# First four blocks of a windowed attention: products of the exponentials in float32 on TensorE instead of split 16-bit values through a DMA transpose; one normalization per half block

## The chip, the cores and the metric

One core of a Trainium2 chip runs the whole program. The metric is device microseconds of one execution; three executions of the kernel before stand at 866.73, 866.99 and 868.85 us.

The engines are PE (TensorE, matrix products; PEld is its loading of the stationary operand), DVE (VectorE), ACT (ScalarE), POOL (GpSimd) and SP (SyncE, which here only issues DMAs). Each runs its own instructions strictly in program order; they wait for one another by semaphores.

## The reference, cut to what matters

```python
# attention: 4 sequences, 8 heads, 576 positions, 64 columns a head
scores = q @ k.T / 8 + slopes[h] * -(i - j)     # where 0 <= i - j < 128, else -1e9
attn = exp(scores - max); attn = attn / (sum(attn) + 1e-9)
x = attn @ v                                    # as 2304 tokens x 512
# dense layer
h = x @ w_in; g = h - tanh(h); x = g @ w_out    # 512 -> 2048 -> 512
# eight experts, each token to the one with the largest cosine
out[token] = gate * (relu(x @ w1[e]) @ w2[e])   # 512 -> 1024 -> 512
```

All of it is float32. Which expert a token goes to hangs on small differences, so the kernel carries nearly all of its products in float32 accuracy, most of them as three products of values split in a high and a low part.

## The kernel before, in words

The 2304 tokens are 18 blocks of 128, two to a group. Attention of a block needs the keys of the block itself and of the one before (a window of 128), so a row of scores has 256 columns, or 128 in block 0. A block is worked in two halves of four heads, and a half in two quarters of two heads; quarters are numbered `a`, 16 of them in blocks 0 to 3. The two heads of a quarter are `jj` 0 and 1, and each has a PSUM tile of its own, `sc0` and `sc1`.

A quarter (function `quarter`) goes through these steps, which give the names in the rows:

- `scores` on PE into `sc` (L437 in blocks 0 to 3, from unsplit float32 `kf` and `qf`; L442 later, from split `khl` and `qst`);
- `soft` on DVE (L464): adds the bias, scales, and takes the row's minimum into `mx`; in an odd block in two pieces of 128 columns, since the previous block's keys stand ahead of the current ones there;
- `exp` on ACT (L477): exponentials into `p32` or `p32x` in float32, and their row sums into `sm`;
- `s_hi` (L482) and `s_lo` (L487): the exponentials as two float16 parts in `ph`, mostly on ACT and POOL;
- `tr` on SP's queue (L492): a transposing DMA into `pt`;
- `pv` on PE (L501): eight short bf16/float16 products into the PSUM tile `o` (four in block 0), against values `vt` that `v_half` split in three bf16 parts (L410 to L416);
- `recip` on DVE (L508, L509), `red` on DVE (L517: sums the three parts of `o` into `xr`), `mul` on DVE (L521).

`x_out` transposes a finished block's `xr` on PE (L566) and splits it into `xT` (L578, L579).

The dense layer goes over groups of two blocks and eight pairs of feature tiles (`step`): 24 matmuls into `h` (L619), tanh and the difference `t` (L624, L627), the split `gh`, `gl` (L632, L636), 12 matmuls into `acc` (L643). The first visits are group 0 with the first four pairs, group 1 with all eight, group 0 with the last four, group 2 and so on.

The weights come as pairs of 32-bit words which the kernel rebuilds into float32 and splits (function `weight`), 32 tiles of 128 x 512 each: a scaling (L306 on ACT or L308 on DVE), L322 on ACT, two integer passes on DVE (L325, L328), the high part (L312, ACT or DVE) and the low part (L316, POOL or DVE). They go through three staging buffers, `wst` (two halves) and `wst2`.

The order of the whole program comes from a planner (`Plan`): each task has engines with a planned cost, keys that it reads and writes, and a due time. The planner takes the task that could start earliest, chooses the engine where there are several, and fixes the order on every engine. Semaphores are added afterwards from the data that instructions share, and any two accesses of one PSUM bank from different engines are put in order.

Of the kernel before, what the change touches and what calls it, by code (L numbers as in the profile page):

```python
# [24 lines left out]
DM = H * D  # L25
# [137 lines left out]
class Builder:  # L163
# [15 lines left out]
    def setup(self):  # L179
# [34 lines left out]
        self.vt = self.at.tile([128, 2, H, 3 * D], BF16, name="vt", bufs=1)  # L214
        self.cum = self.rt.tile([128, E], BF16, name="cum")
# [69 lines left out]
    def weight(self, P, j, kind, f, due):  # L285
# [110 lines left out]

    def v_half(self, P, b, hf, due):
# [21 lines left out]
    def quarter(self, P, a, due):  # L419
# [8 lines left out]
        pb = a % 2 if a < NPX else 0  # L428

        def scores(jj):  # L430
            sc = v["sc"][jj] = self.psA.tile([128, 2, 128], F32, tag=f"sc{jj}", name=f"sc{jj}", bufs=1)
# [3 lines left out]
            if b < NF:  # L435
                for x in [b] if one else [b - 1, b]:
                    nc.tensor.matmul(sc[:, x % 2, :], lhsT=q[p0:p0 + 64, 0, qq, :],  # L437
                                     rhs=self.kf[x % 4 // 2][p0:p0 + 64, x % 2, hf * 2 + qq, :], start=True, stop=True)
# [6 lines left out]
        def soft(jj):  # L445
            t = v["sc"][jj]
            cur, prv = s, 1 - s
# [6 lines left out]
            if one:  # L454
                parts = [(t[:, s, :], 0, 128)]
            elif s == 0:
# [11 lines left out]
        def exp(jj):  # L468
            if "p32" not in v:
                if pb:  # L470
                    v["p32"] = self.wp.tile([128, 1024], F32, tag=f"wi{FT - 1}", name="p32x")
                else:
                    v["p32"] = self.at.tile([128, 512], F32, tag="p32", name="p32", bufs=1)
                v["sm"] = self.at.tile([128, 2], F32, tag=f"sm{a % 4}", name="sm", bufs=1)
            t = v["sc"][jj]
            x = t[:, s, :] if one else t.rearrange("p s t -> p (s t)")
            nc.scalar.activation(out=v["p32"][:, jj * W:(jj + 1) * W], in_=x, func=AF.Exp, scale=-1.0,  # L477
                                 bias=v["mx"][jj][:, 0:1], accum_out=v["sm"][:, jj:jj + 1])
# [14 lines left out]

        def pv(e):
# [11 lines left out]
        def recip(e):  # L506
            sm = v["sm"]
# [6 lines left out]
        def red(e):  # L514
            if qd == 0:
                self.xr[b] = self.at.tile([128, DM], F32, tag="xr", name="xr", bufs=1)
            nc.vector.tensor_reduce(out=xv(), in_=v["o"][:, :, 0:3 * D].rearrange("p h (n d) -> p h d n", n=3),  # L517
                                    axis=AX.X, op=ALU.add)

        def mul(e):  # L520
            nc.vector.tensor_tensor(out=xv(), in0=xv(), in1=v["sm"].unsqueeze(2).to_broadcast([128, 2, D]),  # L521
                                    op=ALU.mult)
# [7 lines left out]
        for jj in range(2):  # L530
            if b < NF:
# [18 lines left out]
        P.add({"DVE": 0.28}, recip, due, r=["at"], w=[("sm", a % 4, 0), ("sm", a % 4, 1)])  # L550
# [796 lines left out]
```

## Time and profile before

| | |
|---|---|
| median of three runs | 866.99 us |
| the profiled execution | 868.54 us, with a span of 866.8 us from its first to its last instruction |
| PE busy | 808.9 us, 93% of the span |
| DVE busy | 610.3 us, 70% |
| ACT busy | 444.5 us, 51% |
| POOL busy | 248.0 us, 29% |

The profile gives for every instruction its start, its duration and what ended the wait before it. Instructions that follow each other on an engine overlap a little in these records, and matmuls much, so that sums of durations are larger than the busy time. A page of the profile cuts the span in 40 slices; from it one sees where an engine is full and where it is not, which a share over the whole span hides.

### The profile page before, as it was taken

How to read it: one execution, taken by the hardware profiler on the slowest of the kernel's cores; microseconds unless marked ns; L12 is line 12 of the kernel's file. 1: busy time of each engine (PE TensorE's matmuls, PEld its weight loads, DVE VectorE, ACT ScalarE, POOL GpSimd, SP SyncE). 2: the span in 40 equal slices, each digit the busy share in tenths (PEclk: the TensorE clock that was granted, in tenths of full speed). 3: DMA queues.
4: the chain of work that ended last, by engine and by line, in shares of the span. 5: the costliest groups of instructions: out<-in, count | busy, mean ns of one | idle time of the engine just before them, and what ended most of it. 6: DMA issues, size and time to landing. Idle time of an engine off the chain costs nothing.

```text
span 866.8 us, 15502 instructions
## 1 busy us (share of the span) xinstructions
PE 808.9 (93%) x5236; PEld 718.7 (83%) x5236; DVE 610.3 (70%) x1678; ACT 444.5 (51%) x1003; POOL 248.0 (29%) x242
## 2 busy tenths in 40 slices
PE   5797877989999999999999999999999999999995
PEld 4685766979888988888898898999879899999994
DVE  7999999888768667777887786477356665656330
ACT  6777776544455445554555544456154544545220
POOL 4575775333324213223232231022110210110111
PEclk9999889999999999999999999999999999999998
DMA  8998624945443224334334413265256655655000
GB/s 205 275 245 257 228 86 128 298 106 132 88 98 98 67 68 98 92 74 104 86 80 102 100 49 45 89 197 183 86 179 220 195 183 172 207 169 171 24 27 30
DMA packets 125465, 115.77 MB, mean 134 GB/s; under 512 B 77877, under 2 KB 92981, under 8 KB 125248
## 3 DMA queue, kind: packets, MB, share of 16 engines
q1 hardware_dynamic: 122240, 105.23, 45.0%
q0 software_dynamic: 3136, 9.46, 3.0%
q8 instruction: 43, 0.70, 0.3%
q14 instruction: 46, 0.38, 0.1%
HBM read 86.33 MB, written 17.48 MB: 120 GB/s over the span
## 4 chain that ended last, share of the span: by engine, by line
PE 57%; DVE 18%; DMA 11%; issue 9%; SPq 2%; ACT 1%; POOL 1%; POOLq 0%; ACTq 0%; DVEq 0%
PE h L619 18%; PE acc L643 16%; PE he L947 7%; PE y L982 5%; DMA pt<-ph 5%; PE o L501 4%; DMA est<-in_w 3%; DMA out<-yo,ix 3%; DVE wst L328 2%; PE sc L442 2%; DVE sc L464 2%; PE y L978 2%; DVE rawi L325 2%; SPq L852 1%; DVE gl L636 1%
## 5 line engine op out<-in xcount | busy, mean ns | idle before, releaser
L619 PE MATMUL h<-xT,wi 128*128 128x256 f32 x1728 | 229.6, 288 | 3.8 <-DVE xT L579 3.8
L619 PEld LDWEIGHTS h<-xT,wi 128*128 128x128 f32 x1728 | 220.9, 194 | 9.1 <-DVE xT L579 4.0
L643 PE MATMUL acc<-wo,gh 128*128 128x512 f32 x576 | 187.8, 407 | 3.0 <-ACT gh L632 2.6
L643 PE MATMUL acc<-wo,gl 128*128 128x512 f32 x288 | 115.4, 401 | 4.2 <-DVE gl L636 4.1
L643 PEld LDWEIGHTS acc<-wo,gh 128*128 128x128 f32 x576 | 101.4, 192 | 18.3 <-ACT gh L632 3.0
L624 ACT ACTIVATE t<-h 128x512 f32<-128x512 f32 x72 | 42.9, 596 | 111.3 <-PE h L619 97.8
L982 PE MATMUL y<-eo,ge 128*128 128x512 f32 x336 | 88.5, 399 | 0.0
L477 ACT ACTIVATE p<-sc,mx 128x256 f32<-128x256 f32 (+1 forms) x128 | 58.9, 463 | 44.7 <-DVE mx L464 42.7
L464 DVE CUSTOM_DVE_ANT_0 sc<-sc,bias 128x128 f32<-128x128 f32 (+1 forms) x144 | 49.9, 360 | 36.3 <-PE sc L442 34.1
L1007 POOL DMA_INDIRECT out<-yo,ix x24 | 23.7, 986 | 177.2 <-PE y L978 61.8
L487 POOL TENSOR_TENSOR ph<-p,ph 128x512 f16<-128x512 f32 (+1 forms) x34 | 40.1, 1179 | 109.4 <-ACT ph L482 74.1
L643 PEld LDWEIGHTS acc<-wo,gl 128*128 128x128 f32 x288 | 55.2, 192 | 17.6 <-DVE gl L636 5.3
L636 DVE TENSOR_TENSOR gl<-t,gh 128x512 fp32r<-128x512 f32 x72 | 65.6, 912 | 4.2 <-ACT gh L632 3.7
L982 PEld LDWEIGHTS y<-eo,ge 128*128 128x128 f32 x336 | 60.0, 188 | 9.8
L501 PE MATMUL o<-vt,pt 128*128 128x128 bf16 (+1 forms) x544 | 54.3, 246 | 12.8 <-DMA pt<-ph 9.9
L881 DVE TENSOR_TENSOR eo<-est,eo 128x512 fp32r<-128x512 f32 x58 | 43.6, 753 | 31.7 <-ACT eo L877 30.5
L969 DVE SCALAR_TENSOR_TENSOR ge<-he,ge 128x256 fp32r<-128x256 f32 x104 | 29.9, 326 | 50.7 <-ACT ge L963 50.7
L501 PEld LDWEIGHTS <-pt 128*128 128x128 f16 x544 | 41.0, 103 | 29.7 <-DMA pt<-ph 17.0
L877 ACT CAST eo<-est 128x512 fp32r<-128x512 f32 x64 | 39.7, 620 | 41.1 <-PE y L978 21.2
L947 PE MATMUL he<-xT,ei 128*128 128x320 f32 x384 | 60.4, 309 | 0.0
L947 PEld LDWEIGHTS he<-xT,ei 128*128 128x128 f32 x384 | 58.3, 188 | 2.3
L947 PE MATMUL he<-xA,ei 128*128 128x320 f32 (+1 forms) x384 | 59.0, 303 | 0.0
(174 smaller groups left out, 1439.5 us busy)
## 6 DMA issues: line engine op xcount, KB each, us to landing
est<-in_w SPq DMA_DIRECT2D x128, 256.0 KB
rawi<-in_w_in SPq DMA_DIRECT2D x16, 512.0 KB
rawo<-in_w_out SPq DMA_DIRECT2D x16, 512.0 KB
stk<-in_k SPq DMA_DIRECT2D x30, 256.0 KB
stq<-in_q SPq DMA_DIRECT2D x28, 256.0 KB
bucket<-in_c_pad SPq DMA_DIRECT2D x8, 771.0 KB
vst<-in_v SPq DMA_DIRECT2D x36, 128.0 KB
xe<-bucket SPq DMA_DIRECT2D x17, 257.0 KB
```

The lines of the kernel that those rows point to most:

```text
L464: nc.vector.tensor_tensor_reduce(out=x, in0=x, in1=self.bias[:, h, c0:c1], scale=-0.125, scalar=mx[:, 1:2] if m else 3.0e38, op0=ALU.add, ...
L477: nc.scalar.activation(out=v["p32"][:, jj * W:(jj + 1) * W], in_=x, func=AF.Exp, scale=-1.0, bias=v["mx"][jj][:, 0:1], accum_out=v["sm"][: ...
L487: self.eng(e).tensor_tensor(out=ph[:, 2 * W:4 * W], in0=v["p32"][:, 0:2 * W], in1=ph[:, 0:2 * W], op=ALU.subtract)
L501: nc.tensor.matmul(o[:, jj, c0:3 * D], lhsT=v["pt"][:, (l * 2 + jj) * KB + kb, :], rhs=self.vt[:, s if one else kb, qd * 2 + jj, 0:3 * D - ...
L619: nc.tensor.matmul(h3(v["h"], f2), lhsT=w[:, a, k, :], rhs=xT[c][:, :, k, :], start=(k == 0 and n == 0), stop=(k == KD - 1 and n == 2))
L624: nc.scalar.activation(out=v["t"], in_=v["h"].rearrange("p a b -> p (a b)"), func=AF.Tanh)
L636: self.eng(e).tensor_tensor(out=v["gl"], in0=v["t"], in1=v["gh"].bitcast(F32), op=ALU.subtract)
L643: nc.tensor.matmul(self.acc[g, t], lhsT=v[a][:, c0:c0 + 128], rhs=self.w["o", fs[f2]][:, c, :], start=(first and f2 == 0 and n == 0), stop ...
L877: nc.scalar.copy(out=t[:, 0, :], in_=v["x"])
L881: self.eng(eng).tensor_tensor(out=t[:, 1, :], in0=v["x"], in1=t[:, 0, :].bitcast(F32), op=ALU.subtract)
L947: nc.tensor.matmul(h[:, 0:N], lhsT=w[:, a, c0:c0 + 128], rhs=xT()[b][:, k, 0:N], start=(k == 0 and n == 0), stop=(k == KD - 1 and n == 2))
L982: nc.tensor.matmul(y[t], lhsT=gt(f, a)[:, (t - ts[0]) * 128:(t - ts[0] + 1) * 128], rhs=self.w["o", f0 + f][:, b, :], start=(f == 0 and n ...
```

## The change

In blocks 0 to 3 (`early`) the exponentials stay in float32. PE transposes them (`tr_pe`, against the identity `ident`, which is part of `con`) into the second half of the PSUM bank that holds the scores; ACT or DVE copies the transposed tile out (`tr_out`, into `ptf`); PE multiplies it with unsplit values `vf` in float32 (`pv_f`). `vf` lies in the slots of two of the last weight tiles (w_in 14 and 13), whose loads wait for it. The four heads of a half now share one PSUM tile `of`, so that one reciprocal and one multiplication serve a half block. In later blocks the reciprocal and the multiplication are also once per half, and POOL may do the multiplication. The score tiles are allocated once, with 512 columns each; in early blocks the current keys always come first, which makes `soft` one piece.

```diff
+        self.scores = [self.psA.tile([128, 2, 2, 128], F32, tag=f"sc{n}", name=f"sc{n}") for n in range(2)]
...
+        elif kind == "i":
+            slots = [("vf", 2 * (FT - 2 - f) + x) for x in range(2)]
...
+    def v_full(self, P, b, due):
+
+        def load(e):
+            if b % 2 == 0:
+                self.vf[b // 2] = self.wp.tile([128, 2, 512], F32, tag=f"wi{FT - 2 - b // 2}", name=f"vf{b // 2}")
+            self.nc.sync.dma_start(out=self.vf[b // 2][:, b % 2, :], in_=self.i["v"][b * 128:(b + 1) * 128, :])
...
+        early = b < NF
+        cs = 0 if early else s
...
+        def tr_pe(jj):
+            t = self.scores[jj][:, 1]
+            for x in range(W // 128):
+                nc.tensor.transpose(t[:, x, :], v["p32"][:, jj * W + x * 128:jj * W + (x + 1) * 128], self.ident)
+
+        def tr_out(e, jj):
+            if jj == 0:
+                v["pt"] = self.at.tile([128, 512], F32, tag=f"pt{a % 2}", name="ptf", bufs=1)
+            t = self.scores[jj][:, 1].rearrange("p s t -> p (s t)")
+            (nc.scalar.copy if e == "ACT" else nc.vector.tensor_copy)(
+                out=v["pt"][:, jj * W:(jj + 1) * W], in_=t[:, 0:W])
+
+        def pv_f(e):
...
+                    nc.tensor.matmul(o[:, qq * 2 + jj, :], lhsT=v["pt"][:, (jj * KB + kb) * 128:(jj * KB + kb + 1) * 128],
+                                     rhs=self.vf[x // 2][:, x % 2, c:c + D], start=(kb == 0), stop=(kb == KB - 1),
+                                     skip_group_check=True)
...
+        if early:
+            for jj in range(2):
+                P.add({"PE": 0.15 if one else 0.25}, lambda e, jj=jj: tr_pe(jj), due, r=["at", "con", ("p32", pb, jj)],
+                      w=[("tp", jj)])
+            for jj in range(2):
+                P.add({"ACT": 0.3, "DVE": 0.22} if one else {"ACT": 0.4, "DVE": 0.35}, lambda e, jj=jj: tr_out(e, jj),
+                      due, r=["at", ("tp", jj)], w=[("pt", a % 2, 1)] if jj else [("pt", a % 2), ("pt", a % 2, 1)])
+            P.add({"PE": 0.6 if one else 1.2}, pv_f, due,
...
+            if qq:
+                P.add({"DVE": 0.5}, recip, due, r=["at"], w=sm)
+                P.add({"DVE": 0.4}, mul, due, r=["at", "o", ("o", 0), ("o", 1)] + sm, w=half if hf else [("xr", m) for m in range(4)])
+            return
...
-        P.add({"DVE": 0.28}, recip, due, r=["at"], w=[("sm", a % 4, 0), ("sm", a % 4, 1)])
...
-        P.add({"DVE": 0.2}, mul, due, r=["at", ("sm", a % 4, 0), ("sm", a % 4, 1)], w=[("xr", qd)])
+        if qq:
+            P.add({"DVE": 0.5}, recip, due, r=["at"], w=sm)
+            P.add({"DVE": 0.5, "POOL": 0.7}, mul, due, r=["at"] + sm, w=half)
...
-                        self.v_half(P, b, hf, due)
+                        if b < NF and hf == 0:
+                            self.v_full(P, b, due)
+                        if b >= NF - 1:
+                            self.v_half(P, b, hf, due)
```

Since the planner sets the order anew, every engine's order moves. The line numbers of the changed kernel are higher: `soft` is L479, the reciprocal L548 and L549, the integer passes on weights L328 and L331. On DVE, at the softmax of block 2's first quarters (`ISA sc` is `soft`, the number behind `sc` is a buffer's), this stood before:

```order
L464 ISA sc_438,mx_470<-sc_438,bias 128x256
L464 ISA mx_470 128x1
L464 ISA sc_447,mx_473<-sc_447,bias 128x256
L464 ISA mx_473 128x1
L517 TENSOR_REDUCE xr<-o 128x128
L328 SCALAR_TENSOR_TENSOR wst<-wst,rawo_380 128x512
L521 TENSOR_TENSOR xr<-xr,sm 128x128
L508 TENSOR_SCALAR sm<-sm 128x2
L509 RECIPROCAL sm<-sm 128x2
L325 SCALAR_TENSOR_TENSOR rawo_419<-rawo_419 128x512
L464 ISA sc_485,mx_511<-sc_485,bias 128x256
```

and at the same place this stands now:

```order
L479 ISA sc_92,mx_428<-sc_92,bias 128x256
L479 ISA mx_428 128x1
L331 SCALAR_TENSOR_TENSOR wst<-wst,rawi_257 128x512
L479 ISA sc_93,mx_443<-sc_93,bias 128x256
L479 ISA mx_443 128x1
L313 CAST wi_446<-wst 128x512
L328 SCALAR_TENSOR_TENSOR rawi_364<-rawi_364 128x512
L567 TENSOR_TENSOR xr<-of,sm 128x256
L328 SCALAR_TENSOR_TENSOR rawo_384<-rawo_384 128x512
L519 COPY ptf<-sc_92 128x256
L479 ISA sc_92,mx_476<-sc_92,bias 128x256
```

The reduction, the small multiplications and reciprocals between two quarters are replaced by more passes on weights, by one multiplication of a half block, and by a copy out of the score bank ahead of the next softmax in that bank.

On PE, between the scores of one early quarter and the next (`sc_508`, `sc_524`), the product was a run of short pairs, of which the last four stand here:

```order
L501 LDWEIGHTS pt
L501 MATMUL o<-vt,pt 128x192
L501 LDWEIGHTS pt
L501 MATMUL o<-vt,pt 128x192
L501 LDWEIGHTS pt
L501 MATMUL o<-vt,pt 128x128
L501 LDWEIGHTS pt
L501 MATMUL o<-vt,pt 128x128
L437 MATMUL sc_508<-kf_124,qf_364 128x128
L437 MATMUL sc_508<-kf_166,qf_364 128x128
L437 MATMUL sc_524<-kf_124,qf_444 128x128
```

Now the transposes of one quarter (L513) stand ahead of the next quarter's scores in each of the two banks, and the product (L530) behind them:

```order
L513 MATMUL sc_92<-con,p_440 128x128 x2
L452 MATMUL sc_92<-kf_126,qf_325 128x128
L452 MATMUL sc_92<-kf_158,qf_325 128x128
L628 MATMUL misc<-con,xr 128x128 x4
L513 MATMUL sc_93<-con,p_440 128x128 x2
L452 MATMUL sc_93<-kf_126,qf_325 128x128
L452 MATMUL sc_93<-kf_158,qf_325 128x128
L530 MATMUL of<-vf_285,ptf 128x64
L530 MATMUL of<-vf_138,ptf 128x64
L530 MATMUL of<-vf_285,ptf 128x64
L530 MATMUL of<-vf_138,ptf 128x64
```

So the next scores of a bank are behind the transposes of the last exponentials, which they were not before.

On DVE, where the last weight tile is finished (`wo_1584` before), the surroundings were those of block 4's attention:

```order
L464 ISA sc_1450,mx_1535<-sc_1450,bias 128x256
L464 ISA mx_1535 128x1
L367 TENSOR_TENSOR qst_1516<-stq,qst_1516 128x512
L636 TENSOR_TENSOR gl<-t,gh 128x512
L328 SCALAR_TENSOR_TENSOR wst<-wst,rawo_1283 128x512
...
L316 TENSOR_TENSOR wo_1584<-wst,wo_1584 128x512
```

Now the last weights (`wi_1216`, `wo_1232`) are finished ahead of block 4's first softmax, and behind the sixth `gl` instead of the ninth:

```order
L317 TENSOR_TENSOR wo_1164<-wst,wo_1164 128x512
L689 TENSOR_TENSOR t<-h,t 128x512
L317 TENSOR_TENSOR wi_1183<-wst,wi_1183 128x512
L331 SCALAR_TENSOR_TENSOR wst<-wst,rawi_924 128x512
L698 TENSOR_TENSOR gl<-t,gh 128x512
L331 SCALAR_TENSOR_TENSOR wst<-wst,rawo_821 128x512
L317 TENSOR_TENSOR wi_1216<-wst,wi_1216 128x512
L317 TENSOR_TENSOR wo_1232<-wst,wo_1232 128x512
L464 MEMSET sc_92 64x128
```

## Rows read from the trace of the kernel before

**Rows 1.** Stretches: start:end, length, busy us and instructions per engine, PEclk, DMA, GB/s

```profile
20.70:145.40 124.70, 100.30 (x569) 84.09 (x569) 120.55 (x246) 90.03 (x197) 78.15 (x59) 0.93 0.73 201
157.10:866.80 709.70, 685.59 (x4546) 616.66 (x4544) 463.86 (x1334) 334.20 (x748) 156.89 (x145) 0.99 0.42 117
```

**Rows 2.** Timeline of DVE at the last weight tile: start us, us, instruction

```profile
144.83 0.68 DVE L316 TENSOR_TENSOR wo<-wst,wo 128x512 fp32r<-128x512 f32 x1
145.43 0.28 DVE L521 TENSOR_TENSOR xr<-xr,sm 128x128 f32<-128x128 f32 x1
```

**Rows 3.** Chain that ended last: start us, us, what

```profile
155.87 2.88 PE h L619 x24
...
187.16 2.77 PE acc L643 x12
```

**Rows 4.** Stretches again, of line L619 alone: busy us and instructions of PE, PEld

```profile
0.00:155.00 155.00, 38.45 (x264) 36.72 (x264) 0.94 0.75 205
```

**Rows 5.** DVE by line and shape, 20.7 to 145.4 us: busy us, mean ns

```profile
L325 DVE SCALAR_TENSOR_TENSOR rawi<-rawi 128x512 int32<-128x512 int32 x15 | 17.7, 1183 | 0.0
L325 DVE SCALAR_TENSOR_TENSOR rawo<-rawo 128x512 int32<-128x512 int32 x16 | 15.0, 948 | 0.0
L328 DVE SCALAR_TENSOR_TENSOR wst<-wst,rawo 128x512 int32<-128x512 int32 x16 | 14.4, 916 | 0.0
L328 DVE SCALAR_TENSOR_TENSOR wst<-wst,rawi 128x512 int32<-128x512 int32 x15 | 13.3, 905 | 0.0
...
L517 DVE TENSOR_REDUCE xr<-o 128x128 f32<-128x384 f32 x15 | 8.3, 550 | 1.8 <-PE o L501 1.6
L521 DVE TENSOR_TENSOR xr<-xr,sm 128x128 f32<-128x128 f32 x14 | 7.9, 563 | 0.0
L508 DVE TENSOR_SCALAR sm<-sm 128x2 f32<-128x2 f32 x14 | 7.2, 514 | 0.0
...
L464 DVE DVE_READ_ACCUMULATOR2_ANT mx<- 128x1 f32 x40 | 5.6, 140 | 0.0
L464 DVE CUSTOM_DVE_ANT_0 sc<-sc,bias 128x256 f32<-128x256 f32 x13 | 5.5, 429 | 0.2
L464 DVE CUSTOM_DVE_ANT_0 sc<-sc,bias,mx 128x128 f32<-128x128 f32 x14 | 5.0, 359 | 0.5
...
L464 DVE CUSTOM_DVE_ANT_0 sc<-sc,bias 128x128 f32<-128x128 f32 x13 | 3.8, 291 | 0.0
...
L509 DVE RECIPROCAL sm<-sm 128x2 f32<-128x2 f32 x14 | 2.3, 166 | 0.5
```

**Rows 6.** The second integer pass on DVE: ns min/median/max, first and last start

```profile
L328 DVE SCALAR_TENSOR_TENSOR wst<-wst,rawi x16: 676/686/1780, 14.5 to 132.6; 128x512 int32<-128x512 int32 x16
```

**Rows 7.** POOL by line and shape, 0 to 145 us: busy us, mean ns | idle

```profile
L487 POOL TENSOR_TENSOR ph<-p,ph 128x512 f16<-128x512 f32 x8 | 10.3, 1286 | 7.0 <-ACT ph L482 7.0
```

**Rows 8.** Timeline of PE at six places: start us, us, instruction [idle before]

```profile
32.98 1.22 PE L437 MATMUL sc<-kf,qf 64*128 64x128 f32 x4 [0.39 <-ACT p32x L477]
...
37.38 1.25 PE L501 MATMUL o<-vt,pt 128*128 128x192 bf16 x8
...
47.11 1.11 PE L566 MATMUL misc<-con,xr 128*128 128x128 f32 x4
...
55.58 0.73 PE L501 MATMUL o<-vt,pt 128*128 128x192 bf16 x8
56.24 0.71 PE L437 MATMUL sc<-kf,qf 64*128 64x128 f32 x4
...
163.89 0.60 PE L566 MATMUL misc<-con,xr 128*128 128x128 f32 x4
...
175.47 1.06 PE L718 MATMUL misc<-enT,xt 128*128 128x8 f32 x8
```

**Rows 9.** ACT by line and shape, 0 to 145 us: busy us, mean ns | idle

```profile
L477 ACT ACTIVATE p<-sc,mx 128x256 f32<-128x256 f32 x17 | 8.0, 469 | 7.0 <-DVE mx L464 7.0
```

**Rows 10.** PE by line and shape, 150 us to the end: busy us, mean ns | idle

```profile
L501 PE MATMUL o<-vt,pt 128*128 128x192 bf16 x212 | 33.0, 249 | 10.3 <-DMA pt<-ph 9.0 <-DVE xr L517 1.1
```

More of the change, by code (lines that the diff above doesn't have):

```diff
@@ L395, in qk_half @@
             P.add({"SP": 0.36}, load_q0, due - 2, r=["at"], w=[("q", n), ("ql", n)])
+    def v_full(self, P, b, due):
[3 more added lines that the diff above has]
+            self.nc.sync.dma_start(out=self.vf[b // 2][:, b % 2, :], in_=self.i["v"][b * 128:(b + 1) * 128, :])
+        P.add({"SP": 0.73}, load, due, r=["at"], w=[("vf", b)] + ([("vf", b + 1)] if b % 2 == 0 else []))
     def v_half(self, P, b, hf, due):
@@ L428, in quarter @@
         pb = a % 2 if a < NPX else 0
+        early = b < NF
+        cs = 0 if early else s
+        sk = (a // 2) % 2
         def scores(jj):
-            sc = v["sc"][jj] = self.psA.tile([128, 2, 128], F32, tag=f"sc{jj}", name=f"sc{jj}", bufs=1)
+            sc = v["sc"][jj] = self.scores[jj][:, 0]
             q = self.qst[n]
@@ L436, in scores @@
                 for x in [b] if one else [b - 1, b]:
-                    nc.tensor.matmul(sc[:, x % 2, :], lhsT=q[p0:p0 + 64, 0, qq, :],
+                    nc.tensor.matmul(sc[:, b - x, :], lhsT=q[p0:p0 + 64, 0, qq, :],
                                      rhs=self.kf[x % 4 // 2][p0:p0 + 64, x % 2, hf * 2 + qq, :], start=True, stop=True)
@@ L492, in tr @@
             nc.sync.dma_start_transpose(out=v["pt"][:, 0:4 * W // 128, :], in_=v["ph"][:, 0:4 * W])
+        def tr_pe(jj):
[9 more added lines that the diff above has]
+        def pv_f(e):
+            KB = W // 128
+            if qq == 0:
+                self.oh4[b, hf] = self.psA.tile([128, 4, D], F32, tag="o", name="of", bufs=1)
+            o = self.oh4[b, hf]
+            for jj in range(2):
+                for kb in range(KB):
+                    x, c = b - kb, (qd * 2 + jj) * D
+                    nc.tensor.matmul(o[:, qq * 2 + jj, :], lhsT=v["pt"][:, (jj * KB + kb) * 128:(jj * KB + kb + 1) * 128],
+                                     rhs=self.vf[x // 2][:, x % 2, c:c + D], start=(kb == 0), stop=(kb == KB - 1),
+                                     skip_group_check=True)
         def pv(e):
@@ L520, in mul @@
         def mul(e):
-            nc.vector.tensor_tensor(out=xv(), in0=xv(), in1=v["sm"].unsqueeze(2).to_broadcast([128, 2, D]),
-                                    op=ALU.mult)
+            if early and hf == 0:
+                self.xr[b] = self.at.tile([128, DM], F32, tag="xr", name="xr", bufs=1)
+            x = self.xr[b][:, hf * 256:(hf + 1) * 256].rearrange("p (h d) -> p h d", d=D)
+            self.eng(e).tensor_tensor(out=x, in0=self.oh4[b, hf] if early else x,
+                                      in1=self.sums[b, hf].unsqueeze(2).to_broadcast([128, 4, D]), op=ALU.mult)
         kv = [s] if one else [0, 1]
@@ L1100, in build @@
         tc, nc = self.tc, self.nc
-        for n in ("kf", "qst", "xr", "acc", "w"):
+        for n in ("kf", "vf", "sums", "oh4", "qst", "xr", "acc", "w"):
             setattr(self, n, {})
```

27 lines of the change are left out of this document (17 added, 10 removed).

## The prediction

> **What bounds the kernel now.** I first cut the span into stretches, because the share of DVE over the whole span says little. From 20.7 to 145.4 us DVE is busy 120.55 of 124.7 us, PE 100.3 and ACT 90; from 157.1 us to the end PE is busy 97% [rows 1]. So there are two stages. In the first, DVE runs the attention of blocks 0 to 3 and rebuilds the weights, and nothing can go faster than it; the second is PE's. The timeline of DVE shows where the first ends: the last weight tile is done at 145.4 us [rows 2].
>
> A common mark on PE is needed to compare the two kernels. I take the first matmul with the last w_in tile: the order puts the same 276 matmuls of L619 ahead of it in both. Of these 264 have started by 155 us [rows 4], and the next run of 24 starts at 155.87 and takes 2.88 us [rows 3], so the mark stands at 155.87 + 1.44 = 157.3 us. Behind it the two programs do nearly the same work.
>
> The timeline of PE adds what PEclk, 0.93 over the first stage, does not place: two matmuls of scores (two records each) take 1.22 us at 33 us and 0.71 us at 56 us, a product of a quarter 1.25 us at 37 us and 0.73 us at 56 us, four transposes 1.11 us at 47 us and 0.60 us at 164 us [rows 8]. Nearly twice: by its durations PE ran at the lower of its two clock levels (1.2 instead of 2.4 GHz) until some point between 48 and 55 us, in quarter 10 or 11 of 16.
>
> **What the change takes from DVE.** From the second quarter of block 1 (about 20.7 us) to the last weight tile I count instructions in both orders and price them by [rows 5].
> - Softmax: before, 13 pieces of 128 columns, 14 second pieces, 13 of 256 (five of them block 4's, which now stand behind the weights) and 40 reads of the accumulator, 3.8 + 5.0 + 5.5 + 5.6 = 19.9 us. Now 21 of 256 columns and 21 reads, 21 x (0.429 + 0.14) = 11.9. That is -8.0.
> - 15 reductions go: -8.3.
> - 14 multiplications (7.9 us) become 6 of a half block that read PSUM. No row has that; the nearest, a 128x256 pass on PSUM, is the softmax piece of 0.43 us; bounds are 0.3 (one of 128 columns) and 0.56. 2.6 us, so -5.3.
> - 14 pairs of reciprocals (7.2 + 2.3) become 6 (4.1): -5.4.
> - 6 copies out of PSUM at the same 0.43: +2.6. The other copies are ACT's, which gives up the splits of exponentials and of three quarters of the early values for them, so that its load about stays; it had 35 us to spare.
> - The planner hands DVE four more casts and scalings of weights, at 0.7 each: +2.8.
> - Only six steps of the dense layer stand ahead of the last weight, not nine: three pairs of a difference and a low part, 0.69 + 0.97 each, -5.0. This is no saving; PE gets the bill below.
>
> Together -26.6 us with 84 instructions fewer. Successive instructions overlap by 0.08 us (0.68 us, but the next starts 0.60 later [rows 2]), so 6.7 us of that were never paid: -19.9.
>
> Then there is POOL. The same integer pass takes 686 ns in the median and up to 1780 [rows 6], and the 62 passes of this stretch take 60.4 us [rows 5] where 62 x 0.686 would be 42.5. The long ones lie beside POOL's work, so 17.9 us are lost to it. POOL is busy 78 us there [rows 1]; the splits of exponentials that go cost it 1.29 us each [rows 7], about 13 of them, and some splits of values. With about 30% of its work gone I take 6 us of relief. Bounds: nothing, and 14 us if each of the 13 had held up a pass by 1.78 - 0.69 = 1.1 us.
> The Trainium skill ("SBUF — State Buffer", section "Who interferes with whom") says that DVE with two SBUF inputs and a reading GpSimd instruction exclude each other, so that the later one blocks until the other ends. By that rule the upper bound would be the value, and the sum below 8 us lower; the row's maximum agrees with it, its median says that most passes do not meet it.
>
> The sixth low part, which releases the next products on PE, stands three instructions ahead of the end: -2. For waits on the longer round trip through the score banks (below) I add 3 us. So that point comes at 145.4 - 19.9 - 6 - 2 + 3 = 120.5 us.
>
> **What PE has to do then.** From there to the mark the new order has 60 matmuls of L643's kind (2.77 us per 12, 13.9), 108 of L619's (2.88 per 24, 13.0) [rows 3], 16 of scores (256 columns like L619's, 0.12 each, 1.9) and three products of a quarter (0.73 each [rows 8], 2.2): 31.0 us. Before, 11.9 us were left at 145.4. The mark comes at 151.5 instead of 157.3 us: -5.8.
>
> Ahead of that point PE's work per quarter changes too. The bf16 product goes (1.25 us low, 0.73 high). Four transposes come, 1.11 or 0.60. The float32 product of 64 columns has no row; four float32 matmuls of 8 columns (logits) take 1.06 us at the high level, four of 128 columns 2 x 0.71 = 1.42, at the low level 2.44 [rows 8]. I take 1.2 and 2.1, close to the middle. With the scores PE then needs 5.65 us a quarter at the low level (3.7 before) and 3.2 at the high one (2.15). DVE's part of one quarter in the new order is about 5.3 us: from block 1's second quarter to block 3's last softmax there are 11 quarters with 38 passes on weights at 0.97, 21 softmaxes at 0.57, 12 copies and multiplications at 0.43, 6 reciprocal pairs at 0.68 and 13 other passes at 0.7, less 115 overlaps of 0.08. So PE is covered by DVE at the high level, and not at the low one.
>
> On SP's queue the 16 transposing DMAs of these blocks go, each of which stood in front of loads and waited for POOL. The loads of w_in 13, 14 and 15 now wait until early quarters release their slots. Between block 3's last multiplication and the first pass on w_in 13 DVE has eleven instructions, seven of them passes on other weights, some 9 us; a load that is later than that would hold DVE by the difference.
>
> **Behind the mark** every half block saves a reciprocal pair and a multiplication, some of which POOL takes. DVE is 65% busy there [rows 1], and of PE's waits ahead of later products only 1.1 us end by DVE, 9.0 by the transposing DMA, which stays [rows 10]. Between 0 and -3 us; I take -1.6.
>
> **Sum.** -5.8 - 1.6 = -7.4 us on the profiled execution, 868.54 to 861.1; its time is 1.55 us above the median of the runs, so for the median 866.99 - 7.4 = 859.6.
>
> **Rivals.**
> 1. *Slower: the round trip through a score bank at the low clock.* Softmax, exponentials, transposes, the next scores and the copy now follow each other in one bank, and the order has DVE's softmax wait for ACT's copy. At the low level: 0.57 + (0.47 [rows 9] + about 0.2 for the row sum) + 0.55 + 1.22 + 0.43 = 3.4 us, and within it PE serves the other bank and a product, 0.55 + 1.22 + 2.1 = 3.9. A round of 7.3 us against DVE's 5.3 makes 11 x 2.0 = 22 us, 19 beyond my 3: 859.6 + 19 = 879. It decides at about 0.95 us of excess a round, that is, if PE stays low for half of the rounds. For it speaks that PE stayed low until quarter 10 before; against it that PE now has more to do in that time. The Trainium skill ("PSUM — Partial Sum Buffer", section "PSUM bank collisions raise a hardware error") demands exactly this order: different engines must not touch one bank of a quadrant at once, even in different columns. By that rule the halves of the score bank give no overlap, and the rounds would come out as here.
> 2. *More: DVE's collisions fall further, and PE is at the high level early.* No stalls (-3) and up to 8 us more relief: 849 to 853, 851 in the middle.
> 3. *No change: attention's gain on DVE is eaten by PE.* If half of the rounds are at the low level, or the product costs the upper bound, 7 us go: 864.4 to 869.6.
>
> **Chances.** Forecast (853 to 864.4) 0.47, rival 2 0.20, rival 3 0.16, rival 1 0.17. A measurement of this kernel tells 0.3%, 2.6 us, from no change; faster by more than that 0.67, within 0.16, slower 0.17. The range of 847 to 870 takes in both bounds of the relief and leaves out most of rival 1.
>
> **What would show it.** Right: DVE full from 20 us to the last weight tile, that tile at 118 to 124 us, the median integer pass still at 0.69 but the mean below 0.97, PE's mark near 151 us. Wrong by rival 1: DVE idle ahead of softmax, put down to ACT's copies or PE's scores, with score pairs at 1.22 us beyond 55 us. Wrong by rival 2: the last tile before 115 us. The sum also fails if loads arrive late for DVE, or if the multiplication on POOL holds up later blocks.

## The result, and the profile after

The changed kernel takes 857.53 us in the median (855.91 to 860.56), the kernel before 866.91 in the same series: a ratio of 0.9894, 95% interval 0.9876 to 0.9911, that is 9.4 us less. The profiled execution took 856.46 us, with a span of 854.8 us. The rest of this section compares the two profiled executions; they lie 12.1 us apart, since that of before was slower than its median and that of after faster.

The mark (the first matmul with the last w_in tile) is found as before: 264 matmuls of L681 lie ahead of a run of 24 that starts at 154.58 us (last row of the timeline of PE below), so it stands at 154.58 + 1.44 = 156.0 us, against 157.3 [rows 3, 4].

Here are stretches of the kernel before that [rows 1] did not cover (start:end, length, busy us and instructions of PE, PEld, DVE, ACT and POOL, PEclk, DMA, GB/s):

```profile
0.00:157.30 157.30, 123.54 (x694) 102.28 (x695) 146.64 (x345) 110.34 (x255) 91.13 (x97) 0.95 0.76 207
157.30:866.80 709.50, 685.39 (x4545) 616.46 (x4543) 463.66 (x1334) 334.20 (x748) 156.89 (x145) 0.99 0.42 117
20.00:40.00 20.00, 16.77 (x76) 13.19 (x76) 19.44 (x60) 14.15 (x38) 9.95 (x9) 1.00 1.15 264
40.00:60.00 20.00, 17.88 (x102) 15.47 (x101) 19.33 (x50) 15.62 (x38) 12.99 (x11) 1.00 1.04 245
```

And the same of the changed kernel:

```profile
0.00:156.00 156.00, 137.24 (x748) 116.56 (x749) 127.03 (x282) 101.89 (x241) 64.24 (x72) 0.95 0.61 193
156.00:854.80 698.80, 683.32 (x4546) 614.67 (x4544) 448.38 (x1244) 335.99 (x749) 167.76 (x156) 1.00 0.42 118
20.00:40.00 20.00, 20.00 (x78) 15.79 (x79) 13.46 (x36) 11.89 (x32) 6.64 (x6) 1.00 0.69 228
40.00:60.00 20.00, 19.70 (x102) 16.59 (x101) 17.11 (x38) 15.94 (x41) 10.65 (x8) 1.00 0.84 278
20.70:126.20 105.50, 94.63 (x500) 80.19 (x500) 93.97 (x166) 77.39 (x175) 55.57 (x41) 0.92 0.55 186
0.00:100.00 100.00, 83.58 (x406) 68.51 (x406) 79.51 (x183) 67.74 (x169) 43.21 (x56) 0.94 0.70 232
```

Read PE's column as a ledger, busy and idle. Up to the mark PE is busy 13.7 us more (123.54 to 137.24) and idle 15.0 us less (33.8 to 18.8), which makes the 1.3 us that the mark moved. Behind it PE is busy 2.1 us less and idle 8.6 us less (24.1 to 15.5): 10.7 us. So nearly the whole gain of these two executions lies behind the mark, where the prediction put 1.6 us of it.

PE's waits behind the mark, by the name of what ended them, add up to 13.9 us before and 5.1 now. The one for the transposing DMA fell from 9.0 to 4.1 us. Those that DVE ended fell from 4.1 to 0.2: besides the 1.1 us of [rows 10] these two of before went, one in the routing of tokens and one in the experts (total us, times, longest):

```profile
PE misc L745 <- DVE oh L735: 1.7, 1, 1.7
PE y L978 <- DVE yo L994: 1.1, 1, 1.1
```

One execution of each kernel was profiled. Six runs below keep nearly this order and this work behind the mark, and there they take 699.4 to 701.9 us, so 698.8 is the short end and 10.7 us the large end of this gain.

From 20 to 60 us the engines have changed places. Before, DVE was busy 38.8 of 40 us; now PE is, 39.7 of 40, and DVE 30.6. The timeline of PE shows one round of a quarter there, from product to product 35.48 - 30.24 = 5.24 us, and the place where the durations halve:

```profile
30.24 1.97 PE L530 MATMUL of<-vf,ptf 128*128 128x64 f32 x8
32.00 0.63 PE L513 MATMUL sc<-con,p 128*128 128x128 f32 x2
32.56 1.22 PE L452 MATMUL sc<-kf,qf 64*128 64x128 f32 x4
33.72 0.69 PE L513 MATMUL sc<-con,p 128*128 128x128 f32 x2
34.33 1.22 PE L452 MATMUL sc<-kf,qf 64*128 64x128 f32 x4
35.48 1.97 PE L530 MATMUL of<-vf,ptf 128*128 128x64 f32 x8
...
52.08 2.79 PE L681 MATMUL h<-xT,wi 128*128 128x256 f32 x12
54.70 1.00 PE L530 MATMUL of<-vf,ptf 128*128 128x64 f32 x8
55.54 0.61 PE L513 MATMUL sc<-con,p 128*128 128x128 f32 x4
56.08 0.72 PE L452 MATMUL sc<-kf,qf 64*128 64x128 f32 x8
...
154.58 3.03 PE L681 MATMUL h<-xT,wi 128*128 128x256 f32 x24
```

PEclk reads 1.00 in both stretches, while products take 1.97 us at 30 us and 1.00 at 54.7. By its durations PE is at the lower of its two levels (1.2 and 2.4 GHz) until the first twelve matmuls of the dense layer, though it hardly rests; the run with one burst below shows what to make of the column. What DVE waits for from 20 to 60 us (total us, times, longest):

```profile
DVE sc L479 <- ACT ptf L519: 4.6, 8, 1.1
DVE ptf L519 <- PE sc L452: 2.0, 2, 1.2
DVE rawi L328 <- ACT rawi L325: 1.1, 1, 1.1
DVE xr L567 <- PE of L530: 0.9, 2, 0.6
```

The end of DVE's stage, its timeline at the last weight tile, which is done at 126.1 us and was at 145.5 [rows 2]:

```profile
123.46 0.68 DVE L698 TENSOR_TENSOR gl<-t,gh 128x512 fp32r<-128x512 f32 x1
...
125.43 0.69 DVE L317 TENSOR_TENSOR wo<-wst,wo 128x512 fp32r<-128x512 f32 x1
```

DVE's groups from 20.7 to 126.2 us (busy us, mean ns | idle before), to be set beside [rows 5]:

```profile
L328 DVE SCALAR_TENSOR_TENSOR rawo<-rawo 128x512 int32<-128x512 int32 x16 | 17.1, 1076 | 0.0
L331 DVE SCALAR_TENSOR_TENSOR wst<-wst,rawi 128x512 int32<-128x512 int32 x15 | 16.2, 1087 | 0.1
L328 DVE SCALAR_TENSOR_TENSOR rawi<-rawi 128x512 int32<-128x512 int32 x14 | 14.2, 1012 | 1.1 <-ACT rawi L325 1.1
L331 DVE SCALAR_TENSOR_TENSOR wst<-wst,rawo 128x512 int32<-128x512 int32 x16 | 13.0, 818 | 0.0
L479 DVE CUSTOM_DVE_ANT_0 sc<-sc,bias 128x256 f32<-128x256 f32 x22 | 9.4, 427 | 4.8 <-ACT ptf L519 4.6
...
L567 DVE TENSOR_TENSOR xr<-of,sm 128x256 f32<-128x256 f32 x7 | 2.9, 415 | 0.9 <-PE of L530 0.9
...
L548 DVE TENSOR_SCALAR sm<-sm 128x4 f32<-128x4 f32 x6 | 1.0, 161 | 0.4 <-ACT p32x L493 0.3
```

And the product of the later blocks from 150 us to the end, to be set beside [rows 10]: PE's waits ahead of it have gone from 10.3 to 4.3 us.

```profile
L541 PE MATMUL o<-vt,pt 128*128 128x192 bf16 x208 | 32.3, 248 | 4.3 <-DMA pt<-ph 4.1
```

### The profile page after: what moved, and what is told of

Same layout as the page of the kernel before. It is cut to its first block, busy times and chain, and to the rows that moved or that the text cites. A ratio compares the mean times of both kernels' runs of the same rounds, so it can differ in the third digit from the quotient of the medians.

```text
span 854.8 us, 15357 instructions
## 1 busy us (share of the span) xinstructions
PE 820.6 (96%) x5292; PEld 731.2 (86%) x5292; DVE 575.4 (67%) x1525; ACT 437.9 (51%) x990; POOL 232.0 (27%) x228
## 4 chain that ended last, share of the span: by engine, by line
PE 73%; DVE 10%; issue 7%; DMA 6%; SPq 2%; ACT 2%; POOL 1%; POOLq 0%; ACTq 0%; DVEq 0%
PE h L681 19%; PE acc L705 17%; PE he L1009 10%; PE y L1044 8%; PE o L541 3%; DMA pt<-ph 3%; PE sc L452 3%; DVE wst L331 2%; DMA out<-yo,ix 2%; PE sc L457 2%; PE y L1040 2%; PE of L530 2%; PE misc L780 1%; SPq L914 1%; PE sc L513 1%
## 5 line engine op out<-in xcount | busy, mean ns | idle before, releaser
L681 PE MATMUL h<-xT,wi 128*128 128x256 f32 x1728 | 228.9, 287 | 0.0
L681 PEld LDWEIGHTS h<-xT,wi 128*128 128x128 f32 x1728 | 220.3, 194 | 5.2 <-issue 0.2
L479 DVE CUSTOM_DVE_ANT_0 sc<-sc,bias 128x256 f32<-128x256 f32 (+1 forms) x144 | 52.4, 375 | 44.4 <-PE sc L457 34.7
L1031 DVE SCALAR_TENSOR_TENSOR ge<-he,ge 128x256 fp32r<-128x256 f32 x104 | 30.0, 326 | 54.7 <-ACT ge L1025 54.6
L1025 ACT ACTIVATE ge<-he 128x320 fp32r<-128x320 f32 (+1 forms) x56 | 24.1, 430 | 71.5 <-PE he L1009 66.3
L1009 PE MATMUL he<-xT,ei 128*128 128x320 f32 x384 | 60.4, 309 | 0.0
L689 DVE TENSOR_TENSOR t<-h,t 128x512 f32<-128x512 f32 x72 | 49.4, 686 | 14.8 <-ACT t L686 14.5
L939 ACT CAST eo<-est 128x512 fp32r<-128x512 f32 x64 | 39.7, 621 | 36.8 <-PE y L1040 22.5
L1009 PEld LDWEIGHTS he<-xA,ei 128*128 128x128 f32 x384 | 56.3, 188 | 2.6
```

Of the source, the lines that this page charges most:

```text
L479: nc.vector.tensor_tensor_reduce(out=x, in0=x, in1=self.bias[:, h, c0:c1], scale=-0.125, scalar=mx[:, 1:2] if m else 3.0e38, op0=ALU.add, ...
L681: nc.tensor.matmul(h3(v["h"], f2), lhsT=w[:, a, k, :], rhs=xT[c][:, :, k, :], start=(k == 0 and n == 0), stop=(k == KD - 1 and n == 2))
L689: nc.vector.tensor_tensor(out=v["t"], in0=v["h"].rearrange("p a b -> p (a b)"), in1=v["t"], op=ALU.subtract)
L939: nc.scalar.copy(out=t[:, 0, :], in_=v["x"])
L1009: nc.tensor.matmul(h[:, 0:N], lhsT=w[:, a, c0:c0 + 128], rhs=xT()[b][:, k, 0:N], start=(k == 0 and n == 0), stop=(k == KD - 1 and n == 2))
L1031: nc.vector.scalar_tensor_tensor(out=g[:, o:o + c1 - c0], in0=hk[f][:, c0:c1], scalar=0.0, in1=g[:, c0:c1].bitcast(F32), op0=ALU.max, op1= ...
```

## The experiments

Ratios are to the kernel before, timed in the same series; the changed kernel's is 0.9894. Two theories were set against the prediction's steps. Theory 1: the late normalization takes work from DVE and so removes PE's waits behind the mark. Theory 2: DVE is free of the weights earlier, so the later blocks get a lead.

**Each part alone.** The early part alone keeps the per-quarter `recip` and `mul` of the later blocks:

```diff
-        if qq:
-            P.add({"DVE": 0.5}, recip, due, r=["at"], w=sm)
-            P.add({"DVE": 0.5, "POOL": 0.7}, mul, due, r=["at"] + sm, w=half)
+        P.add({"DVE": 0.28}, recip, due, r=["at"], w=sq)
...
+        P.add({"DVE": 0.2}, mul, due, r=["at"] + sq, w=[("xr", qd)])
```

> The early part alone: blocks 0 to 3 as in the changed kernel, the later blocks normalized per quarter on DVE as before; the order is planned anew. By the prediction's steps the start gives -5.8 us and the later blocks nothing: 861 us. If the late normalization is what removes PE's waits behind the mark (theory 1): the start's measured -1.3 us alone, 865 to 866 us, with some 9 us of waits of PE for the transposing DMA behind the mark. If an earlier free DVE after the weights gives the later blocks a lead (theory 2): 857 to 859 us, with about 4 us of such waits.

The late part alone puts it into the kernel before, where the early blocks keep theirs:

```diff
+        if early:
+            P.add({"DVE": 0.2}, mul, due, r=["at"] + sq, w=[("xr", qd)])
+        elif qq:
+            P.add({"DVE": 0.5}, recip, due, r=["at"], w=sm)
+            P.add({"DVE": 0.5, "POOL": 0.7}, mul, due, r=["at"] + sm, w=half)
```

> The late part alone: the kernel before, with reciprocal and multiplication once per half block and POOL allowed for the multiplication in blocks 4 to 17. By the prediction's steps -1.6 us (0 to -3): 865.3 us. Theory 1 (late normalization removes the waits behind the mark): 857 to 859 us. Theory 2 (the lead from the start does): 866 to 867 us, no change.

Measured: 863.41 us, ratio 0.994 (0.9926 to 0.9955), and 863.27 us, 0.9946 (0.9931 to 0.9962). The kernel before stands at 868.10 us in this series, so the gains are 4.7 and 4.8 us. Each part gives about half, and the halves add up to the whole, 1.14% to 1.06%, within the intervals. Neither theory had that. The early part's gain is not far from the 5.8 us of the prediction's steps, but not at their place: its mark came 0.3 us earlier, and the rest lies behind it. The marks (157.0 and 155.0 us) and the stretches behind them:

```profile
157.00:862.70 705.70, 683.57 (x4546) 615.11 (x4544) 463.50 (x1332) 335.43 (x751) 155.04 (x143) 0.99 0.43 117
```

of the early part, and of the late part

```profile
155.00:861.80 706.80, 684.52 (x4546) 614.30 (x4544) 447.79 (x1246) 337.34 (x752) 164.13 (x151) 1.00 0.43 117
```

Behind the mark each alone leaves 705.7 and 706.8 us, both together 698.8, and before 709.5. PE still waits 8.4 and 9.3 us for the transposing DMA there, so neither part alone removes these waits.

**Work or order.** The changed kernel's order with the old work in it:

```diff
         def red(e):
             begin()
+            sm = self.sums[b, hf][:, 2 * qq:2 * qq + 2]
...
+            nc.vector.reciprocal(out=sm, in_=sm)
...
+            nc.vector.tensor_tensor(out=xv(), in0=xv(), in1=sm.unsqueeze(2).to_broadcast([128, 2, D]), op=ALU.mult)
```

> The changed kernel in its own order, but with the old work put back into the later blocks: behind each reduction the reciprocal pair and the multiplication of that quarter on DVE, none per half. That adds some 14 us of DVE work spread over blocks 4 to 17. Theory 1 (less work on DVE ahead of softmax is what counts): 863 to 866 us. Theory 2, or a better order by itself: 857 to 859 us.

Then two kernels without POOL's share of the multiplications. One keeps the order:

```diff
-            self.eng(e).tensor_tensor(out=x, in0=self.oh4[b, hf] if early else x,
+            nc.vector.tensor_tensor(out=x, in0=self.oh4[b, hf] if early else x,
```

> The changed kernel in its own order, with every multiplication of a later half block on DVE where the planner had given some to POOL. If POOL's share matters: 1 to 2 us slower. If not, within 1 us of the changed kernel.

In the other the order is planned anew:

```diff
-            P.add({"DVE": 0.5, "POOL": 0.7}, mul, due, r=["at"] + sm, w=half)
+            P.add({"DVE": 0.5}, mul, due, r=["at"] + sm, w=half)
```

> The changed kernel with the multiplication of a later half block planned for DVE alone; the order is planned anew and differs in some hundred places behind the mark, with nearly the same work (in its own order that step moved nothing). If the gain behind the mark comes from less work on DVE: 857 to 859.5 us. If it is the luck of one order: 860 to 864 us.

Measured: old work in the new order 862.34 us, 0.993 (0.9911 to 0.9949), slower than the changed kernel by 0.36% or 3.1 us and between its two expectations; on DVE in the same order 858.42 us, 0.990 (0.9883 to 0.9917), no difference; the same work planned anew 862.54 us, 0.9952 (0.9936 to 0.9967), 0.58% or 5.0 us slower. In the last one the start is as in the changed kernel (mark at 156.1 us, last weight tile at 126.2), and the loss lies behind it, most of it from 300 to 500 us, where PE was busy 197.69 us in the changed kernel:

```profile
156.10:859.80 703.70, 683.94 (x4546) 614.62 (x4544) 447.98 (x1244) 336.66 (x751) 168.82 (x154) 1.00 0.42 117
300.00:500.00 200.00, 194.40 (x1417) 174.71 (x1416) 142.81 (x423) 105.82 (x258) 64.76 (x58) 1.00 0.38 86
```

PE's waits for the transposing DMA are 7.4 us there, 4.8 with the old work in the new order, and 4.1 in the changed kernel:

```profile
PE o L541 <- DMA pt<-ph: 7.4, 8, 1.8
```

So these waits follow the order more than the work, and another order of nearly the same work loses some 5 of the 9.4 us. The waits that DVE ends go rather with the work: 4.1 us before, 2.6 in the early part alone and 2.2 with the old work in the new order; 0.6 in the late part alone, 0.4 with the order planned anew and 0.2 in the changed kernel (1.7 and 1.1 in the two orders of the next paragraph). That is theory 1 for some 2 to 4 us, read from one profile of each and not tested by itself.

**Lead.** Attention of blocks 4 to 17 due a step earlier, in both kernels:

```diff
-                d0 = p - 8 * rate - LEAD + 4 * n * rate
+                d0 = p - 8 * rate - LEAD - (g > N0) + 4 * n * rate
```

> The kernel before, with the attention of blocks 4 to 17 due one step of the dense layer (some 6 us) earlier, and the order planned anew. If PE's 10 us of waits for the transposing DMA behind the mark were only a matter of how far ahead the attention is ordered: these waits fall to 4 us or less, 860 to 862 us. If DVE's work per quarter holds it: 866 to 868 us, waits as before.

> The changed kernel with the same: attention of blocks 4 to 17 due one step earlier. If lead is what counts: the 4 us of waits that are left shrink to 1 or 2, 854 to 856 us. If not: 857 to 859 us.

Measured: 880.29 us (1.0148, 1.0122 to 1.0175) and 876.81 us (1.0116, 1.0099 to 1.0133), outside all four expectations. The waits for the DMA did not fall (9.9 and 7.9 us from 150 us on), and PE lost time in the first stage as well: the mark came at 161.4 and 164.3 us. An earlier due time is no help, then; but the whole order changed with it, so that this is no test of a lead by itself. The last run below is one by chance. Its order behind the mark is on DVE nearly that of the changed kernel, and its last weight tile is done 43 us ahead of its mark instead of 30; the stretch behind takes 699.4 us, with 3.9 us of waits for the DMA. So theory 2 has nothing for it. Within the pair timed here, two other orders, the change is worth 3.5 us by the medians, and single executions of the two overlap.

**POOL's relief.** With the early transposes of each head POOL gets one subtraction more, 32 in all, into a tile that nothing reads:

```diff
         def tr_pe(jj):
             t = self.scores[jj][:, 1]
+            nc.gpsimd.tensor_tensor(out=self.junk, in0=self.bias[:, 0, 0:224], in1=self.bias[:, 1, 0:224],
+                                    op=ALU.subtract)
```

> The changed kernel in its own order, with one more subtraction of two 16-bit inputs (128x224, into a tile that nothing reads) on POOL with each pair of early transposes: 32 in all, estimated at 0.55 us each, together about the 17 us that the splits of exponentials took. By the prediction's relief of 6 us the last weight tile would come 6 us later (at about 132 us; 140 at the upper bound), and the time would be some 3 to 6 us longer. If DVE's idle time ahead of softmax, up to 52 us, hides it, or most integer passes don't meet POOL: below 1 us in the time and in the tile.

Measured: 861.09 us, 0.9918 (0.9902 to 0.9934), by the ratios 2.1 us slower than the changed kernel, with intervals that overlap a little. The subtractions took more time than estimated: POOL is busy 27.2 us more up to the mark (158.6 us), and 22.0 us more (77.54 against 55.57) up to the last weight tile. The two stretches, and the first part of the reciprocal in the second:

```profile
0.00:158.60 158.60, 135.95 (x748) 115.79 (x749) 134.28 (x282) 101.82 (x241) 91.42 (x104) 0.96 0.59 190
20.70:128.80 108.10, 93.71 (x501) 79.77 (x501) 100.74 (x166) 77.76 (x175) 77.54 (x64) 0.94 0.53 183
L551 DVE TENSOR_SCALAR sm<-sm 128x4 f32<-128x4 f32 x6 | 3.0, 503 | 0.0
```

DVE is busy 100.74 us instead of 93.97 up to the last weight tile: 6.8 us for 22.0 us of POOL, 0.31 us for each. The integer passes take 4.4 us of it (64.9 instead of 60.5); the first part of the reciprocal (last line above) takes 503 ns again, where it took 161 in the changed kernel and 514 before. The tile came 2.7 us later, between the two expectations; the other 4 us filled DVE's idle time. The Trainium skill ("SBUF — State Buffer", section "Who interferes with whom") has the two engines exclude each other on their shared ports; the trace agrees that POOL's work lengthens DVE's, on the average by 0.31 of its time.

**The round trip and the bank.** The transposes of blocks 0 to 2 go to two other banks:

```diff
             t = self.scores[jj][:, 1]
+            if a < 12:
+                t = v["tp", jj] = self.psA.tile([128, 2, 128], F32, tag=f"acc{jj}", name="tp", bufs=1)
...
```

> The changed kernel in its own order; the transposes of blocks 0 to 2 go to the PSUM banks of acc0 and acc1, which nothing else uses then, instead of the second half of the score bank, so that next scores, copies and softmax of a head no longer follow each other in one bank. Rival 1's mechanism (the round trip through one bank, 7.3 us a round at the lower clock): DVE's 4.6 us of waits for ACT's copies go, DVE is full from 20 us, and the last weight tile comes 3 to 8 us earlier. If it is PE's work itself at the lower clock level that sets the round of 5.24 us (PE is busy 39.7 of the 40 us from 20 to 60): DVE's waits turn into waits for the scores, the tile stays at 125 to 126 us and the time within 1 us.

Measured: 857.54 us, 0.9896 (0.9878 to 0.9914), no difference. DVE's waits from 20 to 60 us changed their name, from ACT's copy to PE's scores, and did not shrink:

```profile
DVE sc L479 <- PE sc L452: 6.5, 9, 1.3
DVE xr L569 <- PE of L532: 2.9, 3, 1.5
```

PE is busy 40.0 of these 40 us. The bank is not what sets the round there; PE's work is. The rule of the Trainium skill on which rival 1 leaned ("PSUM — Partial Sum Buffer", section "PSUM bank collisions raise a hardware error": no two engines in one bank of a quadrant at once) fits DVE's waits for ACT's copy in one bank; taken away, they gave no time in this stretch. The last weight tile came 2.2 us earlier, which neither expectation has: up to it DVE is busy 2.2 us less (91.82 us against 93.97) and idle as long as before (11.4 against 11.5), so no wait was saved. The mark came 2.2 us earlier too, and behind it that was lost again (701.9 us).

**The clock.** Twelve matmuls of 512 columns ahead of quarter 4's scores, or three ahead of each of ten quarters:

```diff
+            if a == 4 and jj == 0:
+                w = self.psA.tile([128, 4, 128], F32, tag="acc0", name="warm", bufs=1)
+                for _ in range(12):
+                    nc.tensor.matmul(w, lhsT=self.ones, rhs=self.ones.unsqueeze(1).to_broadcast([128, 4, 128]),
+                                     start=True, stop=True)
```

> The changed kernel in its own order, with twelve added 16-bit matmuls of 512 columns (of ones, into an unused bank) ahead of the scores of quarter 4, at about 16 us: some 5 us of PE's time at the lower level. If such dense work raises the clock and PE then stays at the upper level: score pairs of 1.22 us become 0.71, products 1.0 instead of 1.97, DVE becomes the bound, its 9 us of idle time from 20 to 60 us shrink to 3, and the last weight tile comes 1 to 4 us earlier in spite of the added work. If the clock falls back at once: rounds of 5.24 us as before, everything some 4 us later.

> As the run with one burst, but three such matmuls ahead of the first scores of each of the quarters 4 to 13: 1.28 us a quarter at the lower level, 0.64 at the upper. If they keep PE at the upper level: rounds set by DVE's 4.3 to 4.7 us, and the last weight tile 3 to 8 us earlier. If not: rounds of 6.5 us, the tile some 10 us later, the time 5 to 10 us longer.

Measured: 858.23 us, 0.9895 (0.9879 to 0.9912), no difference; and 866.31 us, 0.9987 (0.9968 to 1.0005), 0.93% or 8 us slower than the changed kernel. The timeline of PE with one burst:

```profile
16.28 5.18 PE L453 MATMUL warm<-ones 128*128 128x512 bf16 x12
21.39 0.71 PE L457 MATMUL sc<-kf,qf 64*128 64x128 f32 x4
...
26.26 1.25 PE L535 MATMUL of<-vf,ptf 128*128 128x64 f32 x8
...
29.77 0.44 PE L518 MATMUL sc<-con,p32x 128*128 128x128 f32 x2 [1.38 <-ACT p32x L498]
30.14 0.71 PE L457 MATMUL sc<-kf,qf 64*128 64x128 f32 x4
30.78 1.68 PE L535 MATMUL of<-vf,ptf 128*128 128x64 f32 x8
32.24 0.63 PE L518 MATMUL sc<-con,p 128*128 128x128 f32 x2
32.81 1.22 PE L457 MATMUL sc<-kf,qf 64*128 64x128 f32 x4
```

Behind the burst the durations are those of the upper level, a score pair 0.71 and a product 1.25, and a round is so short that PE waits 1.38 us for DVE's and ACT's part. In the product that follows the durations grow, and PE is back at the lower level for 20 us. Here PEclk shows it, at the same 1.22 and 1.97 us at which it reads 1.00 in the changed kernel:

```profile
33.00:52.00 19.00, 19.00 (x74) 15.13 (x74) 15.15 (x36) 13.34 (x34) 8.39 (x6) 0.50 0.79 260
```

The burst cost 5.2 us and gave 5 back: the last weight tile at 126.2 us, which neither expectation has. Three matmuls a quarter did not raise the level in the profiled execution (score pairs at 1.22 up to 60 us) and made the rounds 6.53 us long. That is the 5.24 us and the 1.28 us of added work, so the round is PE's work once more. One of this run's twelve executions took 858.34 us, the others 865 to 869; it was not profiled, and why it was shorter is open.

**Who bounds the start.** The planner's costs of PE in blocks 0 to 3 set to the trace's at the lower level:

```diff
-                P.add({"PE": 0.4 if one else 0.8}, lambda e, jj=jj: scores(jj), due,
+                P.add({"PE": 0.61 if one else 1.22}, lambda e, jj=jj: scores(jj), due,
...
-            P.add({"PE": 0.6 if one else 1.2}, pv_f, due,
+            P.add({"PE": 1.0 if one else 1.97}, pv_f, due,
```

> The changed kernel with the planner's costs of PE in blocks 0 to 3 set to what the trace shows at the lower clock level (scores 1.22 us a head instead of 0.8, a transposed head 0.63 instead of 0.25, a product 1.97 instead of 1.2), and the order planned anew, so that DVE is given passes on weights while it waits for PE. If DVE's 9 us of idle time before 60 us could be used: the last weight tile 4 to 8 us earlier, and, since PE is full from 100 us on, the time only 0 to 3 us shorter. If PE bounds the start anyway: within 1 us of the changed kernel.

Measured: 872.38 us, 1.0062 (1.005 to 1.0074), 15 us slower than the changed kernel, outside both expectations. The first 100 us, to be set beside the last of the changed kernel's stretches above:

```profile
0.00:100.00 100.00, 72.44 (x276) 56.48 (x277) 90.08 (x181) 67.92 (x163) 52.53 (x64) 0.85 0.65 217
```

DVE's idle time could be used, 10.6 us of it (90.08 against 79.51); but the order then put weights first (57 integer passes by 100 us instead of 48) and attention late, and PE was busy 11.1 us less in that time. The last weight tile came no earlier for it, at 128.6 us, and the mark 15.8 us later, at 171.8:

```profile
0.00:171.80 171.80, 142.78 (x748) 119.92 (x749) 134.27 (x293) 98.81 (x232) 59.74 (x70) 0.90 0.56 175
```

So the loss lies ahead of the mark. PE was idle 10.3 us longer there (29.0 against 18.8) and took 5.5 us more for the same 748 instructions: its durations were those of the lower level from 73 to 100 us, behind waits of up to 3.6 us, where the changed kernel's were at the upper one for most of the time. In the new kernel PE's time at the start is what counts, not DVE's.

## Why the prediction was right, and where it was not

The time was inside the range and near the forecast. The sum behind it was not right: its part up to the mark was off by 4.5 us and its part behind it by 9.1, in opposite directions. That they nearly cancelled is luck. Of the signs that it named for being right, only the median integer pass near 0.69 us came (0.68 to 0.76 by group); DVE was not full from 20 us on, the last tile came behind 124 us, and the mark at 156 instead of 151.

- **DVE's work: the total right, in part by luck.** Predicted -19.9 and -6 of relief, 25.9 us; measured 120.55 to 93.97, 26.6 us, up to the last weight tile, with 80 instructions fewer (84 predicted). Softmax (-7.4 for -8.0), reductions (-8.3), multiplications (-5.0 for -5.3) and copies (+2.9 for +2.6) came as priced. The 6 us of relief did not come where they were put; others made them up: reciprocal pairs fell by 7.4 instead of 5.4 us, casts and scalings rose by 1.3 instead of 2.8, and 2.7 us of clearing score tiles and splitting queries, which the sum left out, went from this stretch.
- **Relief: the step that failed inside that total.** Nearly 23 us of POOL's work are gone from the stretch (78.15 to 55.57 us), but the integer passes take 60.5 us for 61 where they took 60.4 for 62. Their mean, which was to fall below 0.97, is 0.99. The long ones lie with the low parts of the weights, which POOL kept: of the passes above 0.8 us that the timeline shows one by one, all 24 overlap work of POOL, 18 of them mainly a low part; before, all 22 did, 13 of them mainly a low part. Why the low parts hold up more passes now is not shown. A small instruction shows relief: the reciprocal's first part went from 514 to 161 ns, and back to 503 with POOL's added work. The upper bound of 14 us did not come.
- **Stalls of DVE: the first step that failed.** The term was +3 us; DVE's idle time in the stage rose from 4.15 to 11.5 us, +7.4. The last tile came at 126.1 instead of 122.5 us. The text had the mechanism ("PE is covered by DVE at the high level, and not at the low one", 5.65 us a quarter), and PE's pitch was 5.24, but it set PE's 5.65 us against a DVE part of 5.3 us and took the 3 us without a working. DVE's part was shorter than that: it is busy 30.6 of 40 us, 4.0 us a round. Product and transposes at either level were as taken (1.97 and 1.00 for 2.1 and 1.2; 1.3 and 0.61 for 1.11 and 0.60).
- **From that point to the mark: nearly.** 31.0 us predicted from the end of the sixth low part; it ended at 124.1 us, the mark came 31.9 later, 1.5 of it one wait for a transposing DMA. The mark moved 1.3 us, not 5.8.
- **Loads behind the early slots: right.** From 60 to 126 us DVE waited for ACT alone, 2.1 us, and never for a load.
- **Behind the mark: the step that failed most.** "Between 0 and -3 us; I take -1.6"; it was 10.7 in the profiled pair, and some 8 by the medians if the start's share is the same. The step counted the waits of later products that end by DVE (1.1 us), not those in the routing and the experts (1.7 and 1.1), which went as well; and it left those that end by the DMA (9.0) where they were, since that DMA stays. They fell to 4.1. A transposing DMA that is late is only the last link; its issue waits for the splits of the exponentials on DVE and POOL, and these for softmax, in the order that the planner set (from the mark to 600 us SP's queue waited 135.9 us for splits before and 104.3 now; but 28.6 us of its waits are now put down to POOL's multiplications, so that this is an argument and not shown). The runs show this much: the old work in the new order costs 3.1 us, the same work in another order 5.0, and either part alone gives some 5 us.
- **Rival 1** had the place right and the bank wrong. Its round was 7.3 us, measured 5.24; the transposes' own banks changed nothing in the time. Pairs of scores at 1.22 us did come back beyond 55 us (at 68 us). Its price did not come: the stalls cost DVE 4.4 us beyond the 3, not 19. Its sign, DVE idle ahead of softmax for ACT's copies and PE's scores, came all the same, since PE's work set the round.
- **Rivals 2 and 3.** No run came near 849 to 853 us. Rival 3's mechanism, PE's added work eating the gain of the start, is what happened to the start; the gain behind the mark hid it.

What stays open: why this order has fewer waits for the DMA behind the mark than its neighbours, and how much each part would give over many orders. Each part was timed in one order only, and two orders of nearly the same work differ by 5 us.

## What to carry to other kernels

When work moves off the engine that bounds a stage, make the ledger of the engine that receives it as well, busy and idle up to a common mark, at the clock level that it has there; the stage here changed its bound at once. A wait that a profile puts down to a DMA can end earlier although the DMA stays, so the steps that feed it belong to the sum. Where a planner sets the order, the order can make up half of a result of 1%: time a second order of the same work before a part gets the credit.

## What the runs showed of the hardware

- PE was busy all of 20 to 40 us in the early quarters' float32 matmuls and transposes, and its durations stayed at the lower level. They were at the upper one behind twelve matmuls of the dense layer and behind twelve 16-bit ones of 512 columns, and at the lower one again behind a wait of 1.38 us.
- PEclk read 1.00 from 20 to 40 us, where durations were nearly twice those of 55 us. In the run with one burst it read 0.50 from 33 to 52 us at the same durations. So a 1.00 ahead of PE's first rise to the upper level says nothing here, and the durations tell.
- A float32 product of four matmuls of 128 rows and 64 columns takes 1.97 us at the lower and 1.00 at the upper level, 0.8 and 0.7 of what four of 64 rows and 128 columns take (2 x 1.22, 2 x 0.71 in the scores): half the columns, not half the time.
- POOL's added subtraction of 224 16-bit columns took 0.86 us (27.6 us in 32), where 256 float32 columns had taken 0.71 and 0.83 in the splits of block 0 before. The narrower type showed no gain; DVE ran beside it in both, so this is no price of the type alone.
